# Bias rows of the first attention head copied by VectorE instead of sent by a transfer

## The chip, the cores and the metric

The kernel runs on one core of a Trainium2 chip. The metric is the time of one execution on the device in microseconds (us). Three runs of the kernel before gave 923.55, 923.83 and 924.00 us; the median is 923.83 us.

## The reference

Causal attention with a decaying bias over 4 x 8 heads of 576 positions and 64 channels, then a mixture of four dense experts on the 2304 rows of 512 channels that come out:

```python
def _attn_ref(q, k, v, s):
    scores = scale * np.matmul(q, k.transpose(0, 1, 3, 2))
    cum = np.cumsum(np.maximum(s, 0.0), axis=-1)
    bias = -(cum[:, :, :, None] - cum[:, :, None, :])
    scores = np.where(causal, -1000000000.0, scores + np.minimum(bias, 0.0))
    scores = scores - np.max(scores, axis=-1, keepdims=True)
    attn = np.exp(scores)
    attn = attn / (np.sum(attn, axis=-1, keepdims=True) + 1e-09)
    return np.matmul(attn, v)

def _moe_ref(x, domain_probs, w1, w2):
    p = domain_probs / (domain_probs.sum(-1, keepdims=True) + 1e-09)
    for e in range(4):
        h = np.maximum(x @ w1[e], 0.0)
        out += p[:, e:e + 1] * (h @ w2[e])
```

The running sums `cum` enter the scores as two more products: one row of ones against the sums of the keys, and one row of sums of the queries against a row of -1.

## The kernel before, in words

The program has two stages. In the first (to about 270 us) attention is computed head by head, and the layers of expert 0 fill what time TensorE has left. In the second the other three experts run from a ring of operand tiles.

The first eight heads are visited twice: the visits 0 to 7 (h0 to h7 in this text) take the first 320 positions of the heads 0 to 7, so that the rows of the first expert can begin early. For such a visit an operand tile `AB` is filled in float32: rows 0 to 63 hold the query and the key channels side by side (transfer at line 616), and rows 64 and 65 hold the bias rows, (ones, sums) and (sums, -1), which one transfer brings from the tile `cx` (line 634). `cx` has one partition for each head and four planes: ones (written by GpSimd, line 462), the sums (a scan on VectorE, lines 482 and 483), the sums again (a copy on ScalarE, line 486) and -1 (GpSimd, line 463). A score is then one matmul with 66 rows of contraction (line 693), in pieces of 64, 128 and 128 query rows. There are four `AB` tiles, and the visit 4 uses again that of visit 0.

Behind the scores, VectorE adds the mask and takes the row's maximum (707), ScalarE takes the exponential and its sum (715), VectorE or GpSimd add 1e-9 (721), VectorE takes the reciprocal (723), one of three engines multiplies (432 or 430), TensorE transposes (742), ScalarE or VectorE move the result to the operand tile (437, 441), and TensorE multiplies it with the values (793). The first layer of expert 0 is line 888 and its second is line 901.

The order of instructions in the attention stage is set by a planner (class `Sched`): each step is a task with its engines, its costs, its dependences, a priority, and buffers that it takes and gives back. The planner plays a clock forward and lets each free engine emit the ready task of the best priority. What it emits is the program's order on that engine, and each engine then runs its own list in that order, waiting on semaphores. Where TensorE has nothing planned, it emits a small matmul of ones with itself (`keep_warm`, line 456, called "filler of ones" here). All transfers are issued by SyncE (SP), one after the other, in the planned order. From the second stage on the order is written out by hand.

Of the kernel before, what the change touches and what calls it, by code (L numbers as in the profile page):

```python
# [11 lines left out]
F32 = mybir.dt.float32  # L12
F32R = mybir.dt.float32r
AF = mybir.ActivationFunctionType
# [5 lines left out]
B, NH, S, D = 4, 8, 576, 64  # L20
# [3 lines left out]
P = 128  # L24
# [25 lines left out]
def rows(m):  # L50
    return (0, 64) if m == 0 else (128 * m - 64, 128 * m + 64)


def t_pe(n):
    return max(n / 2.4 + 13.5, 110)


def t_pe4(n):
    return max(n / 0.6, 157) + 3
# [6 lines left out]
def t_dve(n):  # L66
    return n / 0.96 + 70
# [255 lines left out]
def body(ctx, tc, qk, vp, s, dp, w1, w1s, w2, w2s, out):  # L323
    nc = tc.nc
    sch = Sched()
# [6 lines left out]
    apool = actx.enter_context(tc.tile_pool(name="att", bufs=1))  # L332
# [15 lines left out]
    def slot(name, shape, dt, pool=hpool):  # L348

        if late.get(name, (None, None))[0] != dt:  # L350
            late[name] = (dt, pool.tile(shape, dt, tag=name, name=f"{name}_{'r' if dt == F32R else 'f'}"))
        return late[name][1]
# [11 lines left out]
    def AB(j, dt=F32R):  # L364
        return AB_raw(j, dt)[:, 64:].rearrange("p (x n) -> p x n", x=2)
# [55 lines left out]
    tok = sch.tok  # L421
# [24 lines left out]
    ones, cum, minus = cx[:, 0], cx[:, 1], cx[:, 3]  # L446
# [3 lines left out]
    ones_bf = nc.const_aps.tensor(1.0, [P, 512], mybir.dt.bfloat16)  # L450
# [28 lines left out]
    s0 = rows(VA - 1)[1]  # L479

    def cumulate(u, w):
        nc.vector.tensor_scalar(s_sb[:, u:w], s_sb[:, u:w], 0.0, 8.0, op0=ALU.max, op1=ALU.mult)
        nc.vector.tensor_tensor_scan(out=cum[:, u:w], data0=ones[:, u:w], data1=s_sb[:, u:w], initial=cum[:, u - 1:u] if u else 0.0, op0=ALU.mult, op1=ALU.add)

    def cum_again(u, w):
        nc.scalar.activation(cx[:, 2, u:w], cum[:, u:w], AF.Copy)

    cumulate(0, s0)
    cum_again(0, s0)
    t_cum2 = sch.add({"DVE": 1850}, lambda e: cumulate(s0, S), prio=T_CUM2 / 4)  # L490
    t_cum2.ready = T_CUM2
    t_cum3 = sch.add({"ACT": t_act(S - s0, False)}, lambda e: cum_again(s0, S), [t_cum2], prio=T_CUM2 / 4)
# [111 lines left out]
    for j, (h, ms) in enumerate(VISITS):  # L604
        base = 1000.0 * (j + 1)
        b, hh = divmod(h, NH)
        o = 64 * (hh % 2)
        ext = rows(ms[-1])[1]
# [3 lines left out]
        pq = first or j < NH + NPQ  # L612

        cut = 64 if ext > 512 else 0
        if first:
            ld = sch.add({"SP": 700}, lambda e, j=j, h=h, ext=ext: nc.sync.dma_start(
                out=AB(j, F32)[0:64, :, 0:ext], in_=qk[h, :, 0:ext].rearrange("(c d) n -> d c n", c=2)),
                prio=base - 1500, take=[("AB", j)], seq="AB", xfer=128 * ext * 4)
            ldv = sch.add({"SP": 450}, lambda e, j=j, h=h, nb=nb, o=o: nc.sync.dma_start(out=tok[f"vz{h % 2}", j][:, :, o:o + 64], in_=vp[h][:, 0:nb]),
                          prio=base - 1300, take=[(f"vz{h % 2}", j)], seq=f"vz{h % 2}", xfer=nb * 128 * 64 * 4)  # L620
        else:
            if pq:
                def f(e, j=j, h=h, ext=ext, q0=q0):
                    nc.sync.dma_start(out=AB(j, F32)[0:64, 1, 0:ext], in_=qk[h, 64:128, 0:ext])
                    nc.sync.dma_start(out=AB(j, F32)[0:64, 0, q0:ext], in_=qk[h, 0:64, q0:ext])
                ld = sch.add({"SP": 800}, f, [firstq.get(j - LA)], prio=base - 1500, take=[("AB", j)], seq="AB", xfer=64 * (2 * ext - q0) * 4)
            else:
                ld = sch.add({"SP": 500}, lambda e, j=j, h=h, ext=ext: nc.sync.dma_start(out=tok["raw", j][:, 0:ext], in_=qk[h, :, 0:ext]),
                             [firstq.get(j - LA)], prio=base - 1500, take=[("raw", j)], seq="raw", xfer=128 * ext * 4)
            ldv = sch.add({"SP": 450}, lambda e, j=j, h=h, nb=nb: nc.sync.dma_start(out=tok["vraw", j][:, 0:nb], in_=vp[h][:, 0:nb]),  # L630
                          [firstq.get(j - LV)], prio=base - 1300, take=[("vraw", j)], seq="vraw", xfer=nb * 128 * 64 * 4)
        ldc = None
        if pq:
            ldc = sch.add({"SP": 690}, lambda e, j=j, h=h, ext=ext: nc.sync.dma_start(out=AB(j, F32)[64:66, :, 0:ext], in_=cx[h:h + 1, :, 0:ext].rearrange("p (r c) n -> p r c n", r=2)),
                          [None if first else t_cum3], prio=base - 1490, xfer=10000, follow=ld)
            ldc.ready = T_CUM

        if first:
            qk_ready = [ld, ldc]
# [37 lines left out]
        for m in ms[1:] if joint else ms:  # L677
            pr = base + PM * m
            a, bb = rows(m)
            n = bb - a  # L680
            c = (j, m)
# [3 lines left out]
            for pi, (j0, j1) in enumerate(pieces):  # L685
                lastp = pi == len(pieces) - 1

                def f(e, j=j, a=a, j0=j0, j1=j1, c=c, pi=pi, ext=ext, pq=pq, h=h):
                    t = tok["S", (c, pi)]
                    if pq:  # L690
                        r = AB(j, F32)
                        w = min(P, ext - a)
                        nc.tensor.matmul(t[0:w, 0:j1 - j0], r[0:66, 0, a:a + w], r[0:66, 1, j0:j1], start=True, stop=True)  # L693
                    else:
                        for x, k in ((0, P), (1, 68)):
                            nc.tensor.matmul(t[:, 0:j1 - j0], AB(j)[0:k, x, a:a + P], tok["KK", j][0:k, x, j0:j1], start=(x == 0), stop=(x == 1))  # L696
                qt = sch.add({"PE": (t_pe4(j1 - j0) if pq else 2 * t_pe(j1 - j0))}, f, qk_ready + [last_q], prio=pr + pi, take=[("S", (c, pi))],
                             give=([("AB", j)] if pq else [("AB", j), ("KK", j)] if o or not joint else []) if lastp and m == ms[-1] else [])
                last_q = qt
                qt.lag = S_LAG  # L700
                qt.act = 0.5 if pq else 0.9
                firstq.setdefault(j, qt)

                def f(e, m=m, n=n, a=a, j0=j0, j1=j1, c=c, pi=pi):
                    mx = tok["mx", c]
                    z = tok[f"a{m}", c]
                    nc.vector.tensor_tensor_reduce(  # L707
                        out=z[0:n, j0:j1], in0=tok["S", (c, pi)][0:n, 0:j1 - j0], in1=mask[0:n, 448 - a + j0:448 - a + j1], scale=-0.125,
                        scalar=1e30 if pi == 0 else mx[0:n, 0:1], op0=ALU.add, op1=ALU.min, accum_out=mx[0:n, pi:pi + 1])
                prev = sch.add({"DVE": t_dve(j1 - j0) + 60 * pi}, f, [qt, prev], prio=pr + pi,  # L710
                               take=[("mx", c), (f"a{m}", c)] if pi == 0 else [], give=[("S", (c, pi))])
# [21 lines left out]
            for pi, blocks in enumerate(tp):  # L733
                lastp = pi == len(tp) - 1
                w0 = 128 * blocks[0]
                w = 128 * len(blocks) if m else 64
# [44 lines left out]
        for r0, r1 in ((max(cut, q0), ext),):  # L781
# [4 lines left out]
            def f(e, j=j, mms=mms, first=first, bk=bk, o=o, c0=cut):  # L786
                t = tok[bk]
                for i, (aT, n, i0, i1) in enumerate(mms):
                    if first:
                        st, mv = tok[f"vz{j % 2}", j][:, n, :], tok["aTf", j][:, n, i0:i1]  # L790
                    else:
# [4 lines left out]
            v = sch.add({"PE": cost}, f, evs + [v_ready] + ([prev_v] if first and o else []), prio=base + PO,  # L796
                        take=[bk] if not (first and o) else [], give=[(f"vz{j % 2}", j), ("aTf", j)] if first else [("V", j), ("par", j)])
# [57 lines left out]
    def load_w(e, which, i, t):  # L855
        nc.sync.dma_start(out=t, in_=(w1 if which == 1 else w2)[e, i])
# [6 lines left out]
    for which in (1, 2):  # L863
        for i in range(4):
            pr = (W1 if which == 1 else W2) + i
            k = (which, i)
            ld = sch.add({"SP": 500}, lambda e, k=k: load_w(0, k[0], k[1], tok["stage", k]), prio=pr - 5500 + WS, take=[("stage", k)], xfer=524288)
            n, lo = 1024 // WH, None
# [36 lines left out]
    for gi, tiles in enumerate(GROUPS0):  # L905
        base = 1e6 + 1000 * gi
        w = P * len(tiles)
# [28 lines left out]
        for ti, tt in enumerate(tiles):  # L936
            k = ("mo", (gi, "t", ti))
            for u0 in range(0, 3 * KF, UN):
# [3 lines left out]
                            prio=base + 10 + ti, take=[k] if u0 == 0 else [])  # L942
# [442 lines left out]
```

## Time and profile before

| | us |
|---|---|
| median of three runs | 923.83 |
| the profiled execution's own time | 924.48 |
| its span, from the first to the last instruction | 922.7 |
| TensorE busy | 915.6 |
| weight loads of TensorE busy | 875.8 |
| VectorE, ScalarE, GpSimd busy | 690.8, 453.2, 485.2 |

The profiled execution is one run of its own; 1.8 us of its time lie outside of the span. Busy time of TensorE is modelled at its ends, so that small waits can lie hidden in it. Times of single instructions are starts from the beginning of the span.

### The profile page before, as it was taken

To read this page: it belongs to the slowest core of one execution; us is meant where nothing else is said; L and a number is where in the kernel's file an instruction comes from. 1 tells how busy PE (TensorE), PEld (TensorE's weight loads), DVE (VectorE), ACT (ScalarE), POOL (GpSimd) and SP (SyncE) were. 2 spreads that over 40 slices of the span, in tenths; PEclk is the share of its full clock that TensorE was granted. 3 is DMA by queue.
4 is the path that set the end of the run, shared out by engine and by line. 5 is a ranking of instruction groups with operands and counts; after the bars stand their busy time and mean duration, and the time that the engine had idled before them with its cause. 6 is when DMAs were issued, how large, how long until landed. Compare 5 with 4: busy or idle time off the path is not lost.

```text
span 922.7 us, 17425 instructions
## 1 busy us (share of the span) xinstructions
PE 915.6 (99%) x6127; PEld 875.8 (95%) x6127; DVE 690.8 (75%) x1656; ACT 453.2 (49%) x1034; POOL 485.2 (53%) x530
## 2 busy tenths in 40 slices
PE   9999999999999999999999999999999999999998
PEld 6789998988898998999999999999999999999998
DVE  7888888888851221478879787978796889678977
ACT  5799998898850110453335342525243433433241
POOL 5788787877726794212634353437144813571222
PEclk9999999999999999999999999999999999999999
DMA  6788877778527956296487547854587457754603
GB/s 154 202 256 218 222 207 224 217 210 228 157 89 241 367 203 228 68 362 230 154 283 241 176 150 245 282 184 140 206 285 230 130 202 249 240 167 147 224 29 121
DMA packets 124984, 188.38 MB, mean 204 GB/s; under 512 B 12208, under 2 KB 101072, under 8 KB 124896
## 3 DMA queue, kind: packets, MB, share of 16 engines
q1 hardware_dynamic: 124896, 187.26, 63.8%
q8 instruction: 49, 0.80, 0.4%
q14 instruction: 39, 0.32, 0.1%
HBM read 143.95 MB, written 29.02 MB: 187 GB/s over the span
## 4 chain that ended last, share of the span: by engine, by line
PE 93%; DVE 2%; ACT 2%; DMA 1%; POOL 1%; issue 0%; SPq 0%; POOLq 0%; ACTq 0%; DVEq 0%
PE pb L1189 29%; PE pb L1199 21%; PE mo L1199 8%; PE mo L888 7%; PE mo L901 5%; PE pv L793 5%; PE pb L901 5%; PE T L742 3%; PE pb L888 3%; PE S L696 3%; PE S L693 2%; PE X L742 1%; DVE a L707 1%; DVE aTl L771 1%; ACT a L715 1%; DMA xf_d<-xr 1%
## 5 line engine op out<-in xcount | busy, mean ns | idle before, releaser
L1189 PE MATMUL pb<-x,w1h 128*128 128x384 f32 x1008 | 256.6, 335 | 0.0
L1189 PEld LDWEIGHTS pb<-x,w1h 128*128 128x128 f32 x1008 | 180.9, 188 | 1.5 <-DVE t L1233 1.4
L1189 PE MATMUL pb<-x,w1l 128*128 128x384 f32 x504 | 168.5, 334 | 0.0
L424 POOL TENSOR_TENSOR hT_r<-t,hT_r 128x768 fp32r<-128x768 f32 x17 | 32.0, 1885 | 252.8 <-PE pb L1189 215.4
L1229 ACT ACTIVATE t<-pb 128x384 f32<-128x384 f32 x144 | 66.3, 486 | 158.8 <-PE pb L1189 150.8
L1293 DVE SCALAR_TENSOR_TENSOR acc<-pb,prob,acc 128x256 f32<-128x256 f32 x288 | 124.7, 473 | 5.2 <-PE pb L1199 4.9
L1199 PE MATMUL pb<-w2h,hT_r 128*128 128x256 f32 x720 | 114.6, 283 | 0.0
L1199 PEld LDWEIGHTS pb<-w2h,hT_r 128*128 128x128 f32 x720 | 99.6, 191 | 0.0
L1233 DVE TENSOR_TENSOR t<-pb,t 128x384 f32<-128x384 f32 x108 | 54.4, 549 | 56.9 <-PE pb L1189 35.5
L1189 PEld LDWEIGHTS pb<-x,w1l 128*128 128x128 f32 x504 | 94.6, 188 | 0.0
L1206 ACT ACTIVATE hT_r<-t 128x768 fp32r<-128x768 f32 x54 | 45.7, 846 | 96.5 <-PE pb L1199 92.8
L1203 DVE SCALAR_TENSOR_TENSOR t<-t 128x768 f32<-128x768 f32 x72 | 88.1, 1224 | 1.7 <-issue 1.6
L715 ACT ACTIVATE a<-a,mx 128x448 f32<-128x448 f32 (+4 forms) x136 | 81.1, 598 | 13.9 <-DVE mx L707 12.9
L888 PE MATMUL mo<-xg,w1h 128*128 128x384 f32 (+1 forms) x320 | 80.1, 323 | 0.0
L432 POOL TENSOR_SCALAR a<-a,sm 128x192 f32<-128x192 f32 (+5 forms) x107 | 60.8, 572 | 32.4 <-DVE sm L723 17.3
L1199 PE MATMUL pb<-w2l,hT_r 128*128 128x256 f32 x360 | 71.5, 283 | 0.0
L1293 DVE SCALAR_TENSOR_TENSOR acc<-mo,prob,acc 128x256 f32<-128x256 f32 x144 | 61.1, 473 | 1.1 <-PE mo L1199 1.1
L1203 DVE SCALAR_TENSOR_TENSOR hT_r<-t,hT_r 128x768 fp32r<-128x768 f32 x54 | 56.8, 1052 | 6.7 <-ACT hT_r L1206 6.2
L707 DVE CUSTOM_DVE_ANT_0 a<-S,mask 128x288 f32<-128x288 f32 (+4 forms) x115 | 51.9, 461 | 10.1 <-PE S L693 5.3
L771 DVE TENSOR_TENSOR aTl<-T,aTh 128x256 fp32r<-128x256 f32 (+2 forms) x104 | 51.5, 501 | 10.2 <-ACT aTh L437 9.2
L888 PEld LDWEIGHTS mo<-xg,w1h 128*128 128x128 f32 x320 | 55.2, 189 | 1.2 <-issue 0.6
L1199 PEld LDWEIGHTS pb<-w2l,hT_r 128*128 128x128 f32 x360 | 55.7, 192 | 0.0
(189 smaller groups left out, 2162.8 us busy)
## 6 DMA issues: line engine op xcount, KB each, us to landing
x<-xs_d SPq DMA_DIRECT2D x68, 768.0 KB
x<-x_d SPq DMA_DIRECT2D x55, 768.0 KB
xs_d<-x SPq DMA_DIRECT2D x12, 768.0 KB
raw<-in_qk_dram SPq DMA_DIRECT2D x24, 288.0 KB
KK<-AB_r SPq DMA_DIRECT2D x24, 288.0 KB
x_d<-xh SPq DMA_DIRECT2D x12, 576.0 KB
xg<-x_d SPq DMA_DIRECT2D x16, 384.0 KB
w1r<-in_w1s_dram SPq DMA_DIRECT2D x6, 1024.0 KB
```

Source lines behind the costliest of these rows:

```text
L432: (nc.gpsimd if e == "POOL" else nc.vector).tensor_scalar(out, in_, scale, 1.0 if bias is None else bias, op0=ALU.mult, op1=ALU.mult if bi ...
L707: nc.vector.tensor_tensor_reduce(out=z[0:n, j0:j1], in0=tok["S", (c, pi)][0:n, 0:j1 - j0], in1=mask[0:n, 448 - a + j0:448 - a + j1], scale ...
L715: nc.scalar.activation(z[0:n, 0:bb], z[0:n, 0:bb], AF.Exp, bias=tok["mx", c][0:n, k:k + 1], scale=-1.0, accum_out=tok["sm", c][0:n])
L771: nc.vector.tensor_tensor(out=dst, in0=src, in1=h_.bitcast(F32), op=ALU.subtract)
L888: nc.tensor.matmul(t[:, 0:w], wl[q][:, dc, o:o + P], xgt[:, l, dc, 0:w], start=(u == 0), stop=(u == 3 * KD - 1))
L901: nc.tensor.matmul(t, ht[:, fc, 128 * ti:128 * ti + 128], wl[fc // 2][:, fc % 2, :], start=(u == 0), stop=(u == 3 * KF - 1))
L1189: nc.tensor.matmul(ts[u][:, 0:TG], wv[wl][:, k, 128 * u:128 * u + 128], x[:, xl_, k, :], start=start and k == 0 and n == 0, stop=k == 1 an ...
L1199: nc.tensor.matmul(ts[t][:, 0:256], h_part(o, hl_)[:, k, 128 * t:128 * t + 128], wv[wl][:, k, :], start=start and k == 0 and n == 0, stop= ...
L1203: (nc.gpsimd if e == "POOL" else nc.vector).scalar_tensor_tensor(out=out, in0=in0, scalar=0.0, in1=in1, op0=ALU.max, op1=op)
L1229: nc.scalar.activation(tmp[name][:, u], ts[u][:, 0:TG], f)
L1233: nc.vector.tensor_tensor(out=tmp[name][:, u], in0=ts[u][:, 0:TG], in1=tmp[name][:, u], op=ALU.add)
L1293: nc.vector.scalar_tensor_tensor(out=a_, in0=ts[t][:, 0:256], scalar=prob[:, tt, e:e + 1], in1=a_, op0=ALU.mult, op1=ALU.add)
```

## The change

The bias rows of visit 0 no longer come by transfer. Before the scan, ScalarE writes constants into the operand tile `AB0`, partitions 64 to 96: -1 in the key half, 0 in the query half, and 1 in the query half of partition 64 (three activations with 320 columns from a constant of ones). After the scan, VectorE copies head 0's sums from partition 0 of `cx` to partition 64 of the key half and to partition 96 of the query half. The scores of visit 0 then contract over 97 rows in place of 66; in the rows 65 to 95 the query half is 0. The copies are a planner's task on VectorE, so the planner orders the whole attention stage anew. The other visits keep their transfers.

```diff
@@ -485,8 +485,16 @@
+    first_ab = slot("AB0", [P, 64 + 2 * S], F32, apool)[:, 64:].rearrange("p (x n) -> p x n", x=2)
+    for x, (p0, p1), v in ((1, (64, 97), -1.0), (0, (64, 97), 0.0), (0, (64, 65), 1.0)):
+        nc.scalar.activation(first_ab[p0:p1, x, 0:s0], ones_bf[p0:p1, 0:s0], AF.Copy, scale=v)
     cumulate(0, s0)
     cum_again(0, s0)
+
+    def first_cum(e):
+        assert tok["AB", 0] == "AB0"
+        for p, x in ((64, 1), (96, 0)):
+            nc.vector.tensor_copy(first_ab[p:p + 1, x, 0:s0], cum[0:1, 0:s0])
@@ -630,10 +638,13 @@
-        if pq:
+        if j == 0:
+            ldc = sch.add({"DVE": 2 * t_dve(s0)}, first_cum, prio=base - 1490, follow=ld)
+        elif pq:
             ldc = sch.add({"SP": 690}, lambda e, j=j, h=h, ext=ext: nc.sync.dma_start(out=AB(j, F32)[64:66, :, 0:ext], in_=cx[h:h + 1, :, 0:ext].rearrange("p (r c) n -> p r c n", r=2)),
                           [None if first else t_cum3], prio=base - 1490, xfer=10000, follow=ld)
             ldc.ready = T_CUM
+        rows_k = 97 if j == 0 else 66
@@ -685,12 +696,12 @@
-                        nc.tensor.matmul(t[0:w, 0:j1 - j0], r[0:66, 0, a:a + w], r[0:66, 1, j0:j1], start=True, stop=True)
+                        nc.tensor.matmul(t[0:w, 0:j1 - j0], r[0:rows_k, 0, a:a + w], r[0:rows_k, 1, j0:j1], start=True, stop=True)
```

On the queue of SP, before, at the program's start (`xr` is the input of the sums, `AB_f` from `in_qk_dram` queries and keys, `hT_f` the values, `AB_f` from `cx` the bias rows):

```order
L449 DMA xr_132<-in_s_dram 32x576
L616 DMA AB_f<-in_qk_dram 64x2x320
L619 DMA hT_f<-in_vp_dram 128x3x64
L616 DMA AB_f<-in_qk_dram 64x2x320
L619 DMA hT_f<-in_vp_dram 128x3x64
L634 DMA AB_f<-cx 2x2x320 x2
L616 DMA AB_f<-in_qk_dram 64x2x320
L634 DMA AB_f<-cx 2x2x320
```

The same place on SP now:

```order
L449 DMA xr_132<-in_s_dram 32x576
L624 DMA AB_f<-in_qk_dram 64x2x320
L627 DMA hT_f<-in_vp_dram 128x3x64
L624 DMA AB_f<-in_qk_dram 64x2x320
L627 DMA hT_f<-in_vp_dram 128x3x64
L644 DMA AB_f<-cx 2x2x320
L624 DMA AB_f<-in_qk_dram 64x2x320
L644 DMA AB_f<-cx 2x2x320
```

One of the two transfers of bias rows is gone, and the rest of the queue stands in the old order up to the loads of visit 7 and the third block of weights behind them.

On TensorE, before, where the scores begin (`mo_103` and `mo_104` are PSUM banks; those from a constant are the filler of ones; the first three rows from `AB_f` are visit 0, the next three visit 1, the last two visit 2):

```order
L456 LDWEIGHTS const-bfloat16-1.0
L456 MATMUL mo_103<-const-bfloat16-1.0 128x256
L693 MATMUL S_97<-AB_f 128x64
L693 MATMUL S_98<-AB_f 128x192
L693 MATMUL X_102<-AB_f 128x320
L693 MATMUL mo_103<-AB_f 128x64
L693 MATMUL mo_104<-AB_f 128x192
L693 MATMUL S_97<-AB_f 128x320
L693 MATMUL S_98<-AB_f 128x64
L693 MATMUL X_102<-AB_f 128x192
```

The same place on TensorE now:

```order
L704 MATMUL S_97<-AB_f 128x64
L704 MATMUL S_98<-AB_f 128x192
L704 MATMUL X_102<-AB_f 128x320
L456 LDWEIGHTS const-bfloat16-1.0
L456 MATMUL mo_103<-const-bfloat16-1.0 128x256
...
L704 MATMUL mo_103<-AB_f 128x64
L704 MATMUL mo_104<-AB_f 128x192
L704 MATMUL S_97<-AB_f 128x320
L753 MATMUL T_99<-idn,a_0_120 128x128
L753 MATMUL T_100<-idn,a_0_122 128x128 x2
L704 MATMUL S_98<-AB_f 128x64
```

Before, 17 fillers of ones stand ahead of visit 0 and none between the visits 0 and 1; now two stand ahead of visit 0 and seven between the two visits, and the first two transposes of visit 0 stand ahead of the scores of visit 2.

On TensorE now, behind the scores of visit 7 (`T_99`, `T_100`, `X_102` and `mo_104` from `idn` are transposes, `pv_101` the product with the values):

```order
L704 MATMUL S_97<-AB_f 128x320
L456 LDWEIGHTS const-bfloat16-1.0
L456 MATMUL S_98<-const-bfloat16-1.0 128x256
...
L753 MATMUL T_99<-idn,a_1_125 128x128 x3
L753 MATMUL mo_104<-idn,a_0_120 128x128
...
L753 MATMUL X_102<-idn,a_0_122 128x128 x2
...
L804 MATMUL pv_101<-hT_f 128x320
```

Nine fillers of ones stand here, in runs of four, one, two and two, among the transposes and products of the visits 4 to 6; before there are two at this place, and five more after the scores of visit 2, where now there is none. Up to the last product with the values TensorE's list holds 343 matmuls of expert 0's first layer, and 329 before.

## Rows read from the trace of the kernel before

**Rows 1.** The page's chain that ended last, shares of the span by engine:
```profile
PE 93%; DVE 2%; ACT 2%; DMA 1%; POOL 1%; issue 0%; SPq 0%; POOLq 0%; ACTq 0%; DVEq 0%
```

**Rows 2.** Waits of TensorE's matmuls up to 290 us: total, times, longest:
```profile
PE T L742 <- DVE aTl L771: 0.8, 1, 0.8
...
PE S L693 <- DMA AB_f<-cx: 0.7, 1, 0.7
PE T L742 <- POOL a L432: 0.5, 1, 0.5
PE pv L793 <- ACT hT_f L437: 0.3, 1, 0.3
PE S L693 <- DVE mx L707: 0.2, 1, 0.2
```

**Rows 3.** Timeline of the start: start, duration, engine, line, operation, [idle before, releaser]:
```profile
3.12 0.81 DVE L483 TENSOR_TENSOR_SCAN cx<-cx,xr 32x320 f32<-32x320 f32 x1
3.15 1.66 POOL L476 MEMSET hT_f<- 128x192 f32 x8
...
3.70 2.22 PE L456 MATMUL mo<-const-bfloat16-1.0 128*128 128x256 bf16 x17
...
3.97 0.47 ACT L486 ACTIVATE cx<-cx 32x320 f32<-32x320 f32 x1 [1.75 <-DVE cx L483]
4.53 1.52 SPq L634 DMA_DIRECT2D AB_f<-cx  x2
...
6.09 0.66 SPq L616 DMA_DIRECT2D AB_f<-in_qk_dram  x1
...
6.59 0.79 PE L693 MATMUL S<-AB_f 66*128 66x64 f32 x4 [0.67 <-DMA AB_f<-cx]
...
7.75 0.71 PE L693 MATMUL mo<-AB_f 66*128 66x64 f32 x4
```

**Rows 4.** Prices on VectorE by shape: busy, mean ns of one:
```profile
L482 DVE TENSOR_SCALAR xr<-xr 32x320 f32<-32x320 f32 x1 | 0.3, 337 | 0.5 <-DMA xr<-in_s_dram 0.5
...
L441 DVE COPY hT_f<-mo 128x256 f32<-128x256 f32 x1 | 0.4, 405 | 0.0
...
L441 DVE COPY hT_f<-T 128x64 f32<-128x64 f32 x1 | 0.2, 198 | 0.0
```

**Rows 5.** Two stretches: busy by engine, clock, DMA share, GB/s moved:
```profile
0.00:2.60 2.60, 1.84 (x5) 0.74 (x6) 1.22 (x16) 1.49 (x2) 2.00 (x9) 1.00 0.11 28
2.60:4.00 1.40, 1.40 (x6) 0.54 (x4) 1.15 (x2) 0.03 (x1) 1.33 (x7) 1.00 0.76 188
```

**Rows 6.** Weight loads of score matmuls by rows of contraction: ns min/median/max:
```profile
L693 PEld LDWEIGHTS S<-AB_f x12: 186/190/192, 6.6 to 12.1; 66*128 66x128 f32 x12
...
L696 PEld LDWEIGHTS S<-KK,AB_r x210: 186/190/196, 69.5 to 258.6; 128*128 128x128 f32 x105
```

**Rows 7.** Timeline of SP's queue, later transfers:
```profile
12.96 1.60 SPq L856 DMA_DIRECT2D stage<-in_w_dram  x2
14.61 0.65 SPq L634 DMA_DIRECT2D AB_f<-cx  x1
...
18.42 0.64 SPq L634 DMA_DIRECT2D AB_f<-cx  x1
```

**Rows 8.** Timeline of 19 to 22 us, where visit 5 begins:
```profile
19.93 1.57 POOL L439 TENSOR_SCALAR w1h<-stage 128x1024 fp32r<-128x1024 f32 x1 [0.41 <-DMA stage<-in_w_dram]
...
20.70 0.98 DVE L432 TENSOR_SCALAR a<-a,sm 128x320 f32<-128x320 f32 x1
...
21.59 0.71 PE L693 MATMUL S<-AB_f 66*128 66x64 f32 x4
```

**Rows 9.** Stretches of the span: us, busy of PE, PEld, DVE, ACT, POOL, clock, DMA share, GB/s:
```profile
14.00:20.00 6.00, 5.84 (x37) 4.47 (x35) 5.37 (x30) 4.70 (x18) 3.27 (x7) 1.00 1.00 274
...
60.00:245.00 185.00, 184.08 (x1242) 169.41 (x1241) 156.29 (x603) 168.86 (x471) 147.37 (x271) 1.00 0.79 218
...
290.00:923.00 633.00, 629.04 (x4283) 618.99 (x4281) 463.83 (x778) 219.72 (x378) 280.07 (x163) 1.00 0.61 205
```

More of the change, by code (lines that the diff above doesn't have):

```diff
@@ L686, in body, with f @@
                 lastp = pi == len(pieces) - 1
-                def f(e, j=j, a=a, j0=j0, j1=j1, c=c, pi=pi, ext=ext, pq=pq, h=h):
+                def f(e, j=j, a=a, j0=j0, j1=j1, c=c, pi=pi, ext=ext, pq=pq, h=h, rows_k=rows_k):
                     t = tok["S", (c, pi)]
```

## The prediction

> **What bounds the kernel now.** I read the chain that ended last first. TensorE holds 93% of it and transfers 1% [rows 1]: a microsecond saved on another engine counts only where TensorE would have waited for it. So the next view is what TensorE waited for up to 290 us [rows 2]: 0.7 us for the bias rows of visit 0 and, behind the first score, 0.8 + 0.5 + 0.3 + 0.2 = 1.8 us in four waits. The third is the table of stretches [rows 9]: from 290 us on weight loads fill 618.99 of 633 us, so nothing is to be won there, and what the first stage ends earlier the program should end earlier. Between 60 and 245 us ScalarE is busy for 168.86 of 185 us and VectorE for 156.29, beside a TensorE that idles for 0.92: attention runs at the limit of three engines there, and the layers of expert 0 fill the rest.
>
> What the change touches is the start [rows 3]. The scan ends at 3.12 + 0.81 = 3.93 us, ScalarE's copy of the sums follows at 3.97, SP issues at 4.53, and TensorE has its first score at 6.59, released by that transfer. From 3.70 on it runs 17 fillers of ones and then waits.
>
> **Removed: the transfer of visit 0.** Two issues take 1.52 us, so one takes 0.76 [rows 3]. From 4.53 on SP issues 22 transfers almost without a gap (the largest is 0.11 us), up to the one at 18.42 [rows 3, 7]. So each later load of this stretch can be issued 0.76 us earlier, the two blocks of weights at 12.96 and the bias rows of visit 5 at 14.61 among them. They matter: from 14 to 20 us the transfers' engines are full, at 274 GB/s [rows 9], GpSimd waits for the second block until 19.93, and visit 5 has its scores only at 21.59 [rows 8].
>
> **Added: three activations and two copies.** ScalarE idled for 1.75 us before 3.97. Three activations at 0.47 (its own copy of 32 x 320, the nearest in shape) are 1.41 us and fit with 0.34 to spare; cost nothing. If each took 0.6, the copy of the sums and SP's queue would be later by about 0.05.
>
> No row shows a copy of one partition on VectorE. The nearest with 320 columns, from and to SBUF, is 337 ns; a copy of 64 columns out of PSUM took 198 and one of 256 took 405, which continued to 320 columns gives 0.47 us [rows 4]. I take 0.34 and keep 0.20 and 0.47 as ends. With 0.04 us from the scan to the copies and again to TensorE (3.93 to 3.97 is such a step), visit 0 starts at 3.93 + 0.04 + 0.68 + 0.04 = 4.69 us, which is 1.90 us earlier; 2.18 and 1.64 at the ends. It can't start later than before by this: nothing in it waits for a transfer that was not waited for already. The queries and keys are there: up to 4.0 us 2.6 x 28 + 1.4 x 188 = 336 KB arrived [rows 5], which is the 73.7 KB of the sums' input, the first 163.8 KB of queries and keys, and the first 98.3 KB of values.
>
> **The 97 rows.** A weight load took 190 ns with 66 rows of contraction and 190 with 128 [rows 6], so 97 rows cost nothing.
>
> **Moved: the order.** This takes most of the start back. Now seven fillers of ones stand between the scores of visit 0 and visit 1. Seventeen of them took 2.22 us, 0.13 each [rows 3], so seven are 0.91. Visit 0's scores take from 6.59 to 7.75, 1.16 us. So visit 1 begins at 4.69 + 1.16 + 0.91 = 6.76, against 7.75: 0.99 us of the 1.90 are left. Its bias rows are now the first in the queue and land when those of visit 0 did, in time for 6.59, so they do not hold it; without the fillers TensorE would wait for them to 6.59 anyway. At the ends of the copy's price visit 1 gains 1.16 or 0.73.
>
> Visit 2's loads come 0.76 us earlier and find TensorE about as much ahead. Up to visit 7 I then go by the fillers: nine stand behind the scores of visit 7 where, behind the first score, seven stood before. That is 2 x 0.13 = 0.26 more, and leaves 0.99 - 0.26 = 0.73. The other way, by SP's queue, gives 0.76 for visit 5 and the weights. I take 0.75 us. The four waits of 1.8 us in all [rows 2] are not in this sum; the new order may lose or add some, and I let the sum stand with -1 and +1 for them.
>
> The profiled execution took 924.48 us; less 0.75 it is 923.73. Its time is 0.65 above the median of the runs, so the median, 923.83, becomes 923.1. With -1 and +1 this case spans 922.1 to 924.1. About 0.2% of the time, 1.85 us, is what a measurement of this kernel can tell from no change: the forecast is a gain too small to be told.
>
> **Rivals.**
>
> *The whole start is kept.* If in the new order no wait of TensorE were left behind the first score, the gain would be 1.90 + 0.91 (the seven fillers of before) + 1.8 (the waits) - 16 x 0.13 (the fillers now) = 2.5 us, so 921.3. For it speaks that up to the last product with values 14 more matmuls of the first layer stand in TensorE's list, so the planner found room for them; against it, that all four waits would have to go at once. It is faster by over 0.2% from a gain of 1.85, so two thirds of the 1.8 us of waits must go. 0.23.
>
> *The transfer was hidden anyway.* Up to 34 us the loads of visits 5 to 7 and the weights, and behind them the exponentials, pace TensorE, and what visits 0 to 4 win is waited for again at visit 5: 923.8. For it speaks the full stretch from 14 to 20 us [rows 9]; against it, that the weights themselves are issued 0.76 us earlier. That the copies do not do what they should (held by the third activation) ends here too: it would have to end after 3.97, and 2.22, where the idle time begins (3.97 - 1.75), + 1.41 is 3.63. 0.14.
>
> *The copies are held by GpSimd.* Beside a GpSimd instruction of 1.57 us a VectorE multiply of 128 x 320 took 0.98 us [rows 8], three times the 0.34 of the like form [rows 4]; at the time of the two copies GpSimd is at its memsets, eight in 1.66 us from 3.15, 0.21 each [rows 3]. If each copy waits for one memset more, it is 0.42 us in all, visit 0 starts at 5.11, and the gain is 0.75 - 0.42 = 0.33: 923.5. Against it: a memset may end just when a copy comes, and what SP's queue gives stays. 0.10. The Trainium skill, "SBUF — State Buffer", section "Who interferes with whom", states that a float32 copy within SBUF can take a port pair that VectorE shares with GpSimd, and that whichever comes second waits for the whole instruction of the other. By that rule the wait is certain where a memset is under way; the row of the multiply agrees, and no row here shows a copy beside a memset.
>
> *Slower: the new order starves the chain of attention.* The place is 60 to 245 us. TensorE runs its list in order; the 14 matmuls more stand ahead of scores and transposes, so ScalarE and VectorE get these later, and at 91% and 84% busy [rows 9] they can't catch up. Then TensorE stands before a transpose that is not ready, as in the wait of 0.8 us for VectorE [rows 2]. Before there is one such wait. It is slower by over 0.2% from 1.85 + 0.75 = 2.6 us of new waits, so from four; four are 3.3 us, less the 0.75: 926.3. For it speaks that the order of the whole stage is new and that of before left only 0.92 us idle there; against it, that a planner with the same rules made both. 0.19.
>
> **How the numbers follow.** The forecast, 923.1, has 0.34, the full start 0.23, the hidden transfer 0.14, the held copies 0.10, the starved chain 0.19. Faster by over 0.2% is the second alone, 0.23; slower is the last, 0.19; within 0.2% are the other three, 0.58. The range reaches to the times of both outer cases, 921.0 to 926.2: it leaves out about half of the slower one, and a twentieth beyond the faster.
>
> **What would show it right or wrong.** The first score at about 4.7 us (5.1 with held copies), and two copies of 0.2 to 0.47 us. The first transfer of bias rows issued at 4.5 with the next load at 5.3 instead of 6.09; the blocks of weights at about 12.2. Visit 1 at about 6.8. Visit 5 at 20.8 or a little earlier instead of 21.59; at 21.5 the transfer was hidden. The product with the values of visit 7 about 0.75 us earlier. Then TensorE's waits from 34 to 290 us: with about 1 us the forecast stands, with none the second case, with several of 0.5 to 1 us before transposes the last. If the second stage itself, from 290 us on, took another time than before, the whole reading would be wrong.

## The result and the profile after

The changed kernel took 929.08 us (median of 10 runs, 927.51 to 934.92), the kernel before 923.86 (10 runs beside it, 923.47 to 924.61): a ratio of 1.0060, 95% interval 1.0048 to 1.0073. It is slower by 5.2 us where 923.1 was forecast, and above the 926.2 at which the range ended.

The start came out as forecast in the profiled execution, which is the second quickest of the ten (927.71 us). The timeline of the start, all engines:

```profile
2.23 1.32 ACT L490 ACTIVATE AB_f<-const-bfloat16-1.0 33x320 f32<-33x320 bf16 x3
...
3.12 0.81 DVE L483 TENSOR_TENSOR_SCAN cx<-cx,xr 32x320 f32<-32x320 f32 x1
3.15 2.01 POOL L476 MEMSET hT_f<- 128x192 f32 x8
...
4.04 0.71 DVE L497 COPY AB_f<-cx 1x320 f32<-1x320 f32 x2
4.54 0.81 SPq L644 DMA_DIRECT2D AB_f<-cx  x1
...
4.86 0.79 PE L704 MATMUL S<-AB_f 97*128 97x64 f32 x4 [0.56 <-DVE AB_f L497]
...
5.39 0.63 SPq L624 DMA_DIRECT2D AB_f<-in_qk_dram  x1
...
6.02 0.95 PE L456 MATMUL mo<-const-bfloat16-1.0 128*128 128x256 bf16 x7
...
6.80 0.71 PE L704 MATMUL mo<-AB_f 66*128 66x64 f32 x4
```

Against [rows 3], the first score comes at 4.86 us instead of 6.59, visit 1 at 6.80 instead of 7.75, and the load behind the bias rows at 5.39 instead of 6.09. The two copies took 0.71 together. GpSimd's memsets grew from 1.66 to 2.01: there the copies held GpSimd, not the other way round. Further on visit 5 has its first scores at 20.13 instead of 21.59, and the last products with the values of the first eight visits start at 32.83 instead of 33.44 us, 0.61 earlier.

What TensorE waited for up to 400 us, in the order of the view (total, times, longest), answers to [rows 2]:

```profile
PE pb L899 <- DMA xg<-x_d: 2.5, 1, 2.5
...
PE S L704 <- DVE AB_f L497: 0.6, 1, 0.6
PE pv L804 <- ACT a L726: 0.5, 1, 0.5
PE pv L804 <- ACT hT_f L437: 0.2, 1, 0.2
```

Nothing in it lies between 34 and 290 us. Between 60 and 245 us TensorE is busy for 184.85 of 185 us, before for 184.08 [rows 9]. The new line is the first: 2.5 us for the operands `xg` of expert 0's last group. It stands at 362 us, in the stretch of which the prediction said that nothing was to be won there. TensorE by stretches around it (busy, granted clock, DMA share, GB/s):

```profile
355.00:359.00 4.00, 4.00 (x19) 1.00 0.38 132
359.00:361.00 2.00, 0.64 (x3) 1.00 0.94 198
361.00:363.00 2.00, 0.81 (x4) 0.88 1.09 379
363.00:365.00 2.00, 2.00 (x9) 0.50 1.08 382
365.00:370.00 5.00, 5.00 (x40) 0.91 1.06 398
```

TensorE idles and then runs on with 0.50 of its clock granted, which is the 1.2 GHz level. Up to here the profiled execution was 1.58 us ahead of the one before: its second-layer matmuls start at 277.06 us against 278.64, and the last run of sixteen ahead of the wait at 354.04 against 355.61. Behind it, it is 3.01 us late: the stage after expert 0 begins at 386.48 instead of 383.47. The difference is 4.6 us. Of it 2.66 are the lateness of that one operand (362.13, where it would have been used at 361.05 - 1.58). The other 1.93 come behind it: from there to the next stage it is 24.35 us, before 22.42. I put them down to the slower clock, which e14 tests.

The transfer was late because of SP's queue. The kernel before, at the end of attention, and then its last loads:

```profile
274.44 0.37 SPq L844 DMA_DIRECT2D x_d<-xh  x1
277.82 0.88 SPq L1009 DMA_DIRECT2D t<-xf_d  x2
278.75 2.00 SPq L881 DMA_DIRECT2D xg<-x_d  x4
280.79 1.62 SPq L1009 DMA_DIRECT2D t<-xf_d  x2
...
330.87 21.51 SPq L1026 DMA_DIRECT2D xs_d<-x  x4
352.47 3.44 SPq L881 DMA_DIRECT2D xg<-x_d  x4
```

The same places of the kernel after:

```profile
275.75 0.37 SPq L855 DMA_DIRECT2D x_d<-xh  x1
279.20 0.37 SPq L1020 DMA_DIRECT2D t<-xf_d  x1
279.63 2.00 SPq L892 DMA_DIRECT2D xg<-x_d  x4
281.67 1.49 SPq L1020 DMA_DIRECT2D t<-xf_d  x3
...
335.57 21.52 SPq L1037 DMA_DIRECT2D xs_d<-x  x4
357.19 2.78 SPq L892 DMA_DIRECT2D xg<-x_d  x4
```

The first row is the store of the last rows that attention makes (`x_d<-xh`). Then GpSimd computes sums of two loaded blocks (`t<-xf_d`), and SP stores them (`xs_d<-x`). The second block used to be loaded ahead of four `xg` loads and now comes behind them, so that the first sum starts later. GpSimd before and after:

```profile
282.27 1.85 POOL L993 TENSOR_TENSOR t<-t 128x768 f32<-128x768 f32 x1 [7.86 <-DMA t<-xf_d]
```

```profile
288.74 1.84 POOL L1004 TENSOR_TENSOR t<-t 128x768 f32<-128x768 f32 x1 [13.02 <-DMA t<-xf_d]
```

The first sum is 6.47 us later. The second is 4.52 later (293.40 instead of 288.88), since before it had to wait 1.91 us for its own blocks, and so it goes on: one more wait for blocks has nearly the same length (4.26 now, 4.06 before), and from there on GpSimd's chain is 4.72 late. SP stands in its queue before stores that wait for this chain, for 21.5 us in both kernels, and the last four `xg` loads stand behind those. They, too, are issued 4.72 us later. The load that TensorE waited for came 4.94 us after its issue (357.19 to 362.13). If it took as long in the kernel before, which is an estimate, the operand was there 3.64 us before its use (352.47 + 4.94 against 361.05), and it is 2.66 us behind it now. That is 6.3 us lost between two single executions. 3.34 went because of the load that slid (from the first `t` load to the last `xg` loads it is 77.99 us instead of 74.65). The other 2.96 went because TensorE is further with expert 0 when attention ends (the first `t` load was issued 0.82 us before the second layer's start, now 2.14 behind it): 1.58 is what TensorE won, and 1.38 is that attention itself ends later. This holds beyond these two profiles. In the four others that keep the old order and its 12 or 17 fillers at the start (e2, e3, e7, e13) the last `x_d<-xh` is issued at 273.08 to 273.48 us, in all eight in the new order at 275.48 to 277.23.

Why did a load slide that the diff does not touch? The steps of this preparation are placed by `spent`, which counts the matmul time of expert 0 that the planner left over. The new plan puts 14 more first-layer matmuls into the attention stage, less is left, and a step at "2.0" now falls behind the `xg` loads. This is read from the program; e2 makes the same shift by hand and gets the same order on SP.

### The profile page after: what moved, and what is told of

Its sections match the earlier page's. It is cut to its first block, busy times and chain, and to the rows that moved or that the text cites. A ratio compares the mean times of both kernels' runs of the same rounds, so it can differ in the third digit from the quotient of the medians.

```text
span 925.9 us, 17471 instructions
## 1 busy us (share of the span) xinstructions
PE 916.9 (99%) x6121; PEld 875.4 (95%) x6121; DVE 691.7 (75%) x1659; ACT 454.5 (49%) x1038; POOL 489.5 (53%) x528
## 4 chain that ended last, share of the span: by engine, by line
PE 86%; POOL 5%; DMA 4%; DVE 1%; SPq 1%; ACT 1%; issue 1%; POOLq 0%; DVEq 0%; ACTq 0%
PE pb L1200 28%; PE pb L1210 21%; PE mo L1210 8%; PE mo L899 6%; PE pv L804 5%; PE mo L912 5%; PE T L753 4%; PE S L707 3%; POOL t L1004 2%; DMA t<-xf_d 2%; POOL x L424 2%; PE S L704 1%; PE X L753 1%; PE pb L899 1%; DMA xs_d<-x 1%
## 5 line engine op out<-in xcount | busy, mean ns | idle before, releaser
L899 PE MATMUL mo<-xg,w1h 128*128 128x384 f32 (+1 forms) x328 | 82.8, 326 | 0.0
L432 POOL TENSOR_SCALAR a<-a,sm 128x320 f32<-128x320 f32 (+5 forms) x122 | 67.1, 555 | 27.7 <-DVE sm L734 12.7
L753 PE MATMUL T<-idn,a 128*128 128x128 f32 x324 | 53.4, 273 | 0.2 <-POOL a L432 0.2
```

The costliest lines, as they stand in the source:

```text
L432: (nc.gpsimd if e == "POOL" else nc.vector).tensor_scalar(out, in_, scale, 1.0 if bias is None else bias, op0=ALU.mult, op1=ALU.mult if bi ...
L753: nc.tensor.transpose(t[:, 128 * k:128 * k + 128], z[:, 128 * x:128 * x + 128], idn)
L899: nc.tensor.matmul(t[:, 0:w], wl[q][:, dc, o:o + P], xgt[:, l, dc, 0:w], start=(u == 0), stop=(u == 3 * KD - 1))
```

## The experiments

The theory after this reading: the loss is the slid load and the lost slack, the attention order itself gains. The rival: the new order of attention, the 97 rows or the copies cost the time. Each time is set beside the kernel before on the same chip (923.77, 923.81 and 923.66 in the three sets).

**One transfer moved back (e5).** The kernel after with

```diff
-for at, part in zip(... else (0.0, 2.0, T_LOAD, T_LOAD + 2.0), order):
+for at, part in zip(... else (0.0, 0.0 if g == 1 else 2.0, T_LOAD, T_LOAD + 2.0), order):
```

> The kernel after, with one transfer moved: on SP's queue the second load of the sums' input (t<-xf_d) stands ahead of the four loads xg<-x_d again, as it did before the change; everything else stays. Theory (the lost time is a load of the second stage that slid behind others on SP, which made GpSimd's chain of sums 4.7 us later and with it the last group's xg loads, for which TensorE then waited 2.5 us and ran on at a lower clock): GpSimd's first sum starts at about 282 us again and not at 288.74, the last xg loads are issued at about 352.5 us, no wait of TensorE is left after 34 us, the granted clock is 1.00 from 359 to 370 us, and the 1.58 us that the first stage ends earlier are kept: 923.86 - 1.6 = 922.3, between 921.9 and 922.8. Rival (the new order of attention, the 97 rows or the copies cost the time themselves): as the kernel after, 927.7 to 929.

Measured: 924.48 (922.98 to 925.92, 11 runs), ratio 1.0008 (0.9999 to 1.0016). This one transfer is worth 4.6 us, the whole loss behind 355 us. But the expected 922.3 was missed by 2.2, and the runs spread over 2.9 us. The profiled execution shows why, on TensorE:

```profile
3.70 0.63 PE L456 MATMUL mo<-const-bfloat16-1.0 128*128 128x256 bf16 x2
4.86 1.41 PE L704 MATMUL S<-AB_f 97*128 97x64 f32 x4 [0.53 <-DVE AB_f L497]
6.06 1.27 PE L704 MATMUL X<-AB_f 97*128 97x320 f32 x2
7.12 1.70 PE L456 MATMUL mo<-const-bfloat16-1.0 128*128 128x256 bf16 x7
8.62 1.16 PE L704 MATMUL mo<-AB_f 66*128 66x64 f32 x4
```

The same four matmuls as after, from the same start at 4.86, take 1.41 us instead of 0.79, the seven fillers 1.70 instead of 0.95, and visit 1 comes at 8.62 instead of 6.80. Each of the nine fillers took 417 to 421 ns here; after, the median was 275. TensorE runs at a lower rate until about 9.4 us. The column of the granted clock (the third last) does not show it; only the durations tell it:

```profile
4.00:9.00 5.00, 4.47 (x18) 1.00 0.48 114
```

So there is a second cause, which the profile of the kernel after did not hold. It comes and goes by execution: the kernels after, e5, e6 and e14 have the same program at the start, and of their four profiles only e5's is slow up to 9.4 us. How often it comes in the runs without a profile is not shown.

**The copies in the old order (e3).** The planner is told that visit 0 still has its transfer:

```diff
-ldc = sch.add({"DVE": 2 * t_dve(s0)}, first_cum, prio=base - 1490, follow=ld)
+ldc = sch.add({"SP": 690}, first_cum, prio=base - 1490, xfer=10000, follow=ld)
+ldc.ready = T_CUM
```

> The kernel after, its copies, constants and 97 rows, but the planner still believes in a transfer on SP for visit 0: all lists of work stand as in the kernel before, and only the transfer itself is gone and the three activations and two copies are there. The second load of the sums' input stands ahead of the xg loads. Theory (the order on SP cost the time): no loss, and little gain, since the 17 fillers of ones stay ahead of visit 0 and end at 5.9 us against 6.59 for the first score before; 0.3 to 0.7 us at the start, of which SP's queue gives the later loads 0.76: 923.2 to 923.7. Rival (copies, constants or the wider contraction cost the time): 925 to 929.

Measured: 923.22 (922.57 to 923.71), ratio 0.9993 (0.9984 to 1.0002): as the theory says. The copies, the constants and the 97 rows cost nothing; by the medians they give about 0.5 us, which the interval does not tell from none. The part of the rival that blames them falls: what costs comes with the new order. The spread is 1.1 us here, with 17 fillers ahead of visit 0.

**Later still, but out of the queue (e6).** The kernel after with

```diff
-spent = 0.0
+spent = -8.0
```

> The kernel after, with all steps of the second stage's preparation placed later by 8 us of matmul work. All four loads of the sums' input now stand behind the first four xg loads, so GpSimd's chain starts no earlier than after the change (288 to 290 us), but the last group's four xg loads stand behind nine stores of sums instead of eleven. Theory in its exact form (what hurts is not that GpSimd is late but that the xg loads queue behind stores that wait for it): the last xg loads are issued at 347 to 350 us, no wait of TensorE there, 922.3, between 921.9 and 923.0. A rival within the theory (GpSimd's lateness itself delays the second stage, at 386 us or before): 924 to 929. Rival from outside (the new order of attention): 927.7 to 929.

Measured: 924.44 (922.65 to 929.4, 12 runs), ratio 1.0008 (0.9997 to 1.0019). GpSimd's first sum starts at 287.80, nearly as late as after, and yet no wait for `xg` is left, because these loads now stand ahead of two of the stores:

```profile
334.76 12.23 SPq L1037 DMA_DIRECT2D xs_d<-x  x2
347.04 2.80 SPq L892 DMA_DIRECT2D xg<-x_d  x4
```

It is the queue that hurts, not GpSimd's lateness in itself. The rest of the expected gain (922.3) is missing as in e5. One run took 929.4; it has no profile, and neither has the run of 934.92 of the kernel after, so what held these two stays open. In e6's profile (923.34) the start is late in another way. The timeline there:

```profile
3.15 1.66 POOL L476 MEMSET hT_f<- 128x192 f32 x8
...
4.04 1.29 DVE L497 COPY AB_f<-cx 1x320 f32<-1x320 f32 x2
...
5.43 0.41 PE L704 MATMUL S<-AB_f 97*128 97x64 f32 x2 [1.10 <-DVE AB_f L497]
```

Now the memsets take 1.66, as before, and the copies 1.29 (943 and 319 ns): GpSimd held VectorE. The ten profiles with the copies fall into these two pairs: 2.01 with 0.71 or 0.72 in five (after, e3, e5, e11, e12), 1.65 or 1.66 with 1.28 or 1.29 in the other five.

**Only SP's order, in the old kernel (e2).** The kernel before with `spent = -2.1`, which moves every step of the preparation and gives SP's queue the order of the kernel after (the second `t` load behind the four `xg` loads, and the `xg` loads of the second group ahead of one store). Nothing changes at the start.

> The kernel before, with its steps of the second stage's preparation placed later by 2.1 us of matmul work, which moves the second load t<-xf_d behind the four loads xg<-x_d on SP's queue, as the change did, and nothing of the start. Theory: GpSimd's chain is 3.2 to 4.7 us later; the last xg loads are issued at 355.5 to 357 us and land 4.9 us later, 360.4 to 361.9, where TensorE needs them at 359.8 (in an execution like the one of e7) to 361.05: a wait of 0 to 2 us and up to 1.9 us behind it at half rate; 924 to 927.5, likeliest 925.5. Rival (the place of that load matters only with the new order of attention): 923.8.

Measured: 925.83 (924.13 to 928.13, 12 runs), ratio 1.0022 (1.0014 to 1.0031). This order costs 2.0 us by itself, near the 925.5 that was called likeliest, and the spread grows from 1.5 to 4.0. In its profile (924.63) the last loads are issued at 355.15 and used from 360.11, 4.96 us later: no slack is left. That an execution then loses more or less by tenths of its timing fits the spread; the profile shows one of the quicker runs only.

**Only GpSimd's chain, in the old kernel (e7).** The kernel before, where one split writes its low part four times:

```diff
+for _ in range(4 if g == 1 and o == 7 else 1):
     sub("POOL", blocks[o][:, 1], raw[d], blocks[o][:, 0].bitcast(F32))
```

> The kernel before, with nothing of the change: on GpSimd the second split of sums writes its low part four times instead of once, which is 3 x 1.84 = 5.5 us more for that chain, and nothing else. Theory (the chain from GpSimd's sums over SP's stores to the last xg loads has 3.6 us of slack before, and past that TensorE waits and runs at a lower clock): the last xg loads are issued at about 358 us and land at about 362.9, TensorE waits about 1.9 us from 361.05 on, and the stretch behind it loses 1 to 2 us more at a lower granted clock: 923.86 + 1.9 + 1.5 = 927.3, between 926 and 928.5. Rival (GpSimd's chain has slack enough and the loss of the change lies elsewhere): 923.9.

Measured: 927.31 (927.09 to 928.44, 5 runs), ratio 1.0040 (1.0028 to 1.0052). The time is the one expected, the place is not. TensorE, in this run:

```profile
328.77 0.62 PE L888 MATMUL pb<-xg,w1h 128*128 128x384 f32 x2 [1.83 <-DMA xg<-x_d]
329.22 0.33 PE L888 MATMUL pb<-xg,w1l 128*128 128x384 f32 x1
329.86 1.01 PE L888 MATMUL pb<-xg,w1h 128*128 128x384 f32 x2 [0.30 <-DMA xg<-x_d]
```

That the time agrees is luck in part, for the wait came one group earlier, for the `xg` loads of the second group, which stand behind a store there too. That pushed TensorE back, so the last group's loads, issued at 357.47, were in time. The granted clock fell to 0.50 from 331 to 333 us. So the chain is close to being late at two places, and the mechanism is that of the theory: nothing of the change is in this kernel.

**The fillers, in the old kernel (e10).** The kernel before without 15 of the 17 fillers ahead of visit 0:

```diff
+fills = []
...
+fills.append(0)
+if not 2 < len(fills) <= 17:
     nc.tensor.matmul(b[1][:, 0:256], ones_bf[:, 0:128], ones_bf[:, 0:256], start=True, stop=True)
```

> The kernel before, with 15 of the 17 fillers of ones ahead of visit 0 left out, and nothing else. TensorE then idles from about 4.3 to 6.59 us, where the transfer of the bias rows releases visit 0. Theory (the fillers ahead of visit 0 are what brings TensorE to its full rate in time): the scores of visits 0 and 1 take up to twice as long in part of the executions, the start loses 0 to 2.5 us, median 924.3 to 926, spread 2.5 us or more against 1.8 of before. Rival (fillers don't matter for the clock of the first visits): 923.5 to 923.9, with a spread as before.

Measured: 927.98 (927.63 to 928.25, 5 runs), ratio 1.0045 (1.0032 to 1.0058). The direction was expected; the size is larger, and every run pays it. TensorE there:

```profile
3.70 0.63 PE L460 MATMUL mo<-const-bfloat16-1.0 128*128 128x256 bf16 x2
6.58 1.41 PE L697 MATMUL S<-AB_f 66*128 66x64 f32 x4 [2.25 <-DMA AB_f<-cx]
7.79 1.27 PE L697 MATMUL X<-AB_f 66*128 66x320 f32 x2
8.85 1.27 PE L697 MATMUL mo<-AB_f 66*128 66x64 f32 x4
```

Visit 0 starts at the same time as in [rows 3], its first four scores take 1.41 us instead of 0.79, and visit 1 begins 1.10 us later; the transposes come down from 0.42 to 0.27 only at 15.5 us. 15 matmuls that compute nothing are worth 4.2 us.

**Fillers through the wait (e8), ten fillers (e9).** e5 with 3 or 10 more fillers of ones directly ahead of visit 0:

```diff
+if j == 0 and a == 0 and pi == 0:
+    for _ in range(3):   # e9: 10
+        nc.tensor.matmul(mo[1][:, 0:256], ones_bf[:, 0:128], ones_bf[:, 0:256], start=True, stop=True)
```

> The kernel after with the second load of the sums' input forward, as in e5_second_load_forward, and three more fillers of ones directly ahead of the scores of visit 0, which fill TensorE's wait of 0.5 us for the copies. Theory (e5's median of 924.48 and its spread of 2.9 us come from the start: with two fillers and a wait ahead of visit 0, TensorE is in some executions still at half its rate, as in e5's profile, where all nine fillers took 417 to 421 ns and visit 0 1.41 us instead of 0.79): no wait of TensorE ahead of visit 0, fillers of 273 ns at the latest from about 6 us on, median 922.6 to 923.4, and a spread of 1.5 us or less. Rival (the spread comes from the waits of attention further on): as e5, 924.5, spread 3 us.

> As e8, but ten fillers more ahead of visit 0 instead of three, which end at about 5.2 us at the full rate and 6.3 at half. Theory: TensorE is at its full rate when visit 0 begins or soon behind it, spread 1.5 us or less; the start itself is 0.5 to 1.5 us later than the best start of e5: median 923.2 to 923.9. Rival: as e5 plus the fillers, 925, spread 3 us.

Measured: e8 924.57 (922.79 to 928.26), ratio 1.0010 (0.9999 to 1.0021): a miss, with a spread of 5.5, wider than e5's. In its profile the copies took 1.29, and 0.76 us of the wait was left open. e9 923.83 (922.57 to 925.38), ratio 1.0000 (0.9991 to 1.0008): the median is in the range, the spread, 2.8, is not. In e9's profile TensorE's matmuls do not wait behind 34 us, but its weight loads wait four times for the last `xg`, 1.1 us in all; the loads were issued at 354.23 and used from 359.26, 5.0 us later. The slack of the new order, with the slid load back, is nil. With one of the two mended (e6, e9) a spread remains.

**Both mended (e11), and without the seven fillers (e12).** e11 is e6 with e9's ten fillers; e12 leaves out the seven between visits 0 and 1 as well.

> The kernel after with both suspected costs taken away: ten fillers of ones more ahead of visit 0 (as e9) and the steps of the second stage's preparation 8 us later (as e6), so that the last xg loads stand ahead of two stores. Theory (two causes: a start at half rate in part of the executions, and a chain over GpSimd and SP that has lost its slack): no wait for xg, a full rate from visit 0 on, median 922.5 to 923.1, spread 1.5 us or less, where e6 alone had 924.44 and 3 us and e9 alone 923.83 and 2.8 us. Rival (something else in the new order of attention varies): 923.8 or more, spread 3 us.

> As e11, and without the seven fillers of ones between the scores of visits 0 and 1. Visit 1 follows visit 0 directly, at 6.0 us, and waits for its bias rows up to 6.6, against 7.4 us with the fillers. Theory: 0.7 us less than e11 if nothing later waits, 921.9 to 922.6. Rival (the visits behind are paced by the bias rows and exponentials, so what visit 1 gains is waited for again): as e11.

Measured: e11 923.22 (922.56 to 924.47), ratio 0.9996 (0.9987 to 1.0004); e12 923.10 (922.53 to 923.35), ratio 0.9992 (0.9983 to 1.0001). With both taken away the new order is 5.9 us better than the kernel after, and the spread falls from 2.9 (without the one run at 934.92) to 1.9 and 0.8. For e11 the theory gave 1.5 or less and a median up to 923.1; both are missed by a little. e12's further 0.7 did not come; of it 0.1 is seen. Most of the ten fillers are slow in its profile (1.92 us in all, 1.67 in e11), so visit 0 begins at 5.88. Visit 1 comes at 6.97 instead of 7.51 in e11, but the second layer starts at 277.25 against 277.05: what visit 1 wins is waited for again.

**Twelve fillers in the old order (e13).** e3 without the last five of its 17 fillers.

> As e3_copies_old_plan (the copies, in the order of the kernel before), with 12 fillers of ones ahead of visit 0 instead of 17. They end at 5.2 us at the full rate and at 6.2 at half. Visit 0 starts at 5.2 to 5.6 us instead of 6.37, visit 1 waits for its bias rows up to 6.6 instead of 7.45. Theory (the gain of the copies is real and is kept where the order and the slack behind it are left alone): 0.3 to 0.8 us less than e3, 922.4 to 922.9, spread 1.5 us or less; the GpSimd chain has 3 us of slack, so no wait there. Rival (e3's start gives no more): 923.2.

Measured: 923.34 (922.77 to 923.95), ratio 0.9994 (0.9985 to 1.0003). The rival holds: visit 0 starts at 5.42 instead of 6.37 and visit 1 at 6.59 instead of 7.45, and then visit 2 waits for its queries and keys, which it did not in e3:

```profile
8.38 0.41 PE L709 MATMUL S<-AB_f 66*128 66x64 f32 x2 [0.47 <-DMA AB_f<-in_qk_dram]
```

**The clock behind the late wait (e14).** The kernel after with 24 fillers of ones ahead of the matmul that waits at 359.5 us:

```diff
+if (x[1], x[2], x[3]) == (0, 256, 0):
+    for _ in range(24):
+        nc.tensor.matmul(bank(x[5])[:, 0:256], ones_bf[:, 0:128], ones_bf[:, 0:256], start=True, stop=True)
 l1_mm(x[1], x[2], bank(x[5]), x[3], x[3] + UN)
```

> The kernel after, with 24 fillers of ones (0.11 us each at the full rate, 2.7 us in all) directly ahead of the first matmul that waits for the last xg loads, at about 359.5 us. They do no needed work; they fill the wait of 2.5 us. Theory (of the 4.6 us lost there 2.66 are the wait and 1.93 are TensorE running on at half its rate behind it): the granted clock stays at 1.00 from 359 to 370 us and the 1.9 us are not lost: 929.1 - 1.9 = 927.2, between 926.7 and 927.8. Rival (the stretch behind the wait is slow for another reason, such as the contention of transfers): 929 or more.

Measured: 926.81 (925.91 to 928.48, 6 runs), ratio 1.0035 (1.0024 to 1.0047), 2.3 us less than the kernel after. TensorE by stretches:

```profile
359.00:361.00 2.00, 2.00 (x18) 1.00 0.97 240
361.00:363.00 2.00, 1.94 (x16) 1.00 1.09 374
363.00:365.00 2.00, 1.77 (x13) 1.00 1.07 393
365.00:370.00 5.00, 5.00 (x44) 1.00 1.01 378
```

The transfers' engines are as full as after, and TensorE's granted clock stays at 1.00 behind the wait. The rival falls.

## Why the prediction was wrong

- **"from 290 us on ... nothing is to be won there, and what the first stage ends earlier the program should end earlier."** This step failed: the sum has no term for a loss behind 290 us. That TensorE hardly idles in a stretch says that little is to be won; it does not say how close the loads behind it are to being late. About 3.6 us of slack stood there, which the row of [rows 9] does not show and SP's queue does. The new plan took 6.3 and cost 4.6 us, by the profile and by e5. Nor did attention end earlier: its last rows go out 1.3 us later than in the profile before.
- **The fillers as a price of 0.13 us each.** This term failed too. The prediction counted fillers only as work that is in the way; that 15 fewer stand ahead of visit 0 cost nothing in its sum. e10 shows that they are also what brings TensorE to its full rate. Visit 1 was worked out for 6.76 us and came at 6.80 in the profiled execution, but at 8.62 in e5's. The Trainium skill, "TensorE: Matmul & The Clock Gate", section "Part 1: The HAM clock gate", states that the slow clock is the default and activity releases it, and that the same kernel warms at a different point from run to run. The two durations of one filler, 417 to 421 ns in e5's profile and 273 in the kernel after, agree; the rule spoke against this change and was not weighed.
- **The copies.** 0.34 us each was right (335 and 348 ns), and so was the rival that GpSimd holds them, as one of two outcomes: 0.57 us in all where 0.42 was worked out. It was not one memset for each copy: in e6 the first copy was held for 0.62 us (943 ns instead of 319), about three memsets of 0.21, and the second not at all. The rule of the Trainium skill ("SBUF — State Buffer", "Who interferes with whom") that whichever comes second waits agrees on both sides, with 943 ns for a copy and 433 instead of 258 for a memset; that it waits for one instruction only does not fit the 0.62.
- **The 97 rows cost nothing** (0.79 us for the first four scores in both kernels), **the activations fit** (1.32 us, and ScalarE's copy of the sums at 3.97 in both).
- **The gain of 0.75 us.** Where the rest is left alone it is 0.3 to 0.6 us by the medians of e3, e11, e12 and e13, none of which its interval tells from no gain. The last products of the first eight visits came 0.61 us earlier in the profile, where 0.75 was worked out; visit 5 came 1.46 earlier. From 34 to 290 us no wait was left, which by the prediction's own signs points to the rival in which the whole start is kept. The 1.58 us between the two profiles overstate it: e7, whose first stage is that of the kernel before, reached the second layer at 277.39, 1.25 us ahead of the profile before.
- **The slower rival.** 0.19 was given to it, and only its direction came true: its time (926.3) is 2.8 us short, and its place was wrong, since no wait of TensorE came between 34 and 290 us. The 0.19 stood on another mechanism; that a slower outcome was foreseen at all is luck. The forecast named the stretch from 290 us on as what would overthrow the whole reading, and that is what it did.

Of the loss, 4.6 us go with the one load (e5). e5 is still 0.7 us above the kernel before, and e11 is 0.4 below it: this 1.1 us belongs to the slow start and to the slack that is nil, together. Against the kernel before, e6 stands at +0.7 and e9 at 0.0, so more of it seems to be the start, but each of these medians is good to some 0.8 to 1.0 us, and the runs don't split it reliably. No version here beats the kernel before by more than the measurement can tell; e12 comes nearest to it, 0.56 us below the kernel before.

## What to carry to other kernels

A stage in which the bound engine never waits can still be lost: read how long before its use each operand lands, and which waiting stores its load is queued behind, before a plan's counters are allowed to move it. Matmuls that compute nothing may hold the clock; before one is moved behind real work, look at the durations of the same matmul in the first microseconds, in more than one execution. And set a gain between two single profiles against the spread of the executions before it is believed.

## What was not expected of the hardware

- The column of the granted clock read 1.00 from 4 to 9 us in e5, where every filler took 417 to 421 ns instead of 273, and 0.50 in the late stretch after, where matmuls took 0.41 us instead of 0.28. The durations tell where the column doesn't.
- An idle time of 2.5 us ahead of the late matmul was followed by a granted clock of 0.50 (after), one of 1.83 us too (e7), and with 24 matmuls without use in its place the clock stayed at 1.00 (e14). In e10, where the two fillers at the start were slow already (417 to 421 ns), 2.25 us of idle time was followed by nearly 9 us at the lower rate.
- Two small copies of one partition and eight memsets on another engine meet in one of two ways, execution by execution: 0.71 with 2.01 us, or 1.29 with 1.66. The kernels after and e14 have the same start, and their profiles show one pair each.
